# A fixed order list for an attention and two-MLP kernel, a guard in three tasks, norm steps on ScalarE, and a hinted last branch

## The chip, the cores and the metric

The kernel runs on one core of one Trainium2 chip. The metric is the device time of one execution in microseconds (us), as a median over runs; lower is better.

## What is computed

The reference is a gated linear recurrence (four batches, eight heads, 768 tokens, 48 channels a head), and then two MLPs on its output of 768 x 384 a batch. In the first, `u` and `v` are the two halves of `gelu(x @ w_in)`, `v` is normalised over its 512 columns, mixed over the tokens with a 768 x 768 matrix and multiplied by `u`; in the second, a three-tap convolution over the tokens gates the hidden layer.

```python
state = f[:, :, t, :, None] * state + np.einsum('bhd,bhe->bhde', k[:, :, t], v[:, :, t])
y[:, :, t] = np.einsum('bhd,bhde->bhe', q[:, :, t], state)
...
v_n = (v - mu) / np.sqrt(var + 1e-06) * g_ln
v_s = np.einsum('ts,bsd->btd', w_sg, v_n) + b_sg[None, :, None]
x = x + (u * v_s) @ w_out
...
h = np.maximum(x @ w_in2, 0.0)
return (h * sigmoid(conv3(h, conv_w))) @ w_out2
```

## The kernel before

**Stages.** The recurrence is cut into 24 units of 128 tokens, six a batch (`Attention.plan`). A unit runs two scans of the decays on VectorE (`forth`, `back`), scales k and q (`scale`), turns k on TensorE (`turn_k`) and then runs four sets of 32 small matmuls that use a part of the array each: `update`, `states`, `scores`, `values`. They are called the small matmuls below. Its output goes to a DRAM buffer `xd`. Six units make a batch, and `Mlp.first` takes it up: `L` loads a half batch, `vpart` (v0 to v5) makes one block of 128 tokens of v and normalises it, `upart` makes a block of u, `sg` mixes the tokens, `out1` adds the result to `xd` with an accumulating DMA. Every matmul of the MLPs is made of three passes over a high and a low part of its operands (`mm3`), which use the whole array; `split` makes the two parts of an operand, the high one on ScalarE and the low one by a subtraction on VectorE. `sg` needs all six normalised blocks of its batch. `Mlp.second` does the second MLP in eight half batches: eight `in2_part` and three `out2` each.

**Weights.** Weights arrive in double precision. `narrow` brings a piece to single precision in one step on ScalarE and six on VectorE (L577 to L589), each of which reads what the one before wrote. `w_in` has six pieces of 512 columns (0 to 2 for v, 3 to 5 for u), `w_out` four of 384 (13 to 16), the convolution's weights are piece 12, with 24 columns.

**Order.** Nothing is scheduled on the chip. Every operation is a task (`Order.add`) with an engine, a duration, the tasks that it comes after and the ring slots that it takes, and `Order.run` writes the tasks out one by one; an engine executes its instructions in the order written, and waits at each for what it needs. `Order.run` picks the next task by a cost model of its own (`HOP`, `DMA_RATE`, `TABLE_TIME` and a duration for each task) and by due times from a table (`DUE`). PSUM has three banks of a ring `M` for the MLPs and, once the recurrence is done, five of a ring `MA`.

**The norm.** A block's norm goes to and fro between ScalarE and GpSimd: `gelu` with a sum (L906), `mean` on GpSimd (L909), `square` with a sum (L912), `root` in two GpSimd instructions (L918, and the power at L919), `off` on GpSimd (L922), `norm` (L925).

**Guard.** A flag tells whether the products of the decays stayed large enough; if not, a general path recomputes everything. `switch`, one VectorE task, closes the recurrence's memory, reduces the products, and sets the flag. After the last task the flag is read on every engine (L1468), and each engine branches over the general path (L1470).

Of the kernel before, what the change touches and what calls it, by code (L numbers as in the profile page):

```python
# [8 lines left out]
F32 = mybir.dt.float32  # L9
# [14 lines left out]
P = 128  # L24
# [24 lines left out]
HOP = 0.13  # L49

SLACK = 0.2
DMA_RATE, DMA_TIME, TABLE_TIME = 0.21, 1.9, 1.28
# [4 lines left out]
class Hold:  # L57


    def __init__(self):  # L60
        self.left, self.end = 0, 0.0


class Task:
    __slots__ = ("eng", "us", "fn", "after", "rank", "take", "uses", "hold", "table", "kb", "end", "wait", "nexts", "n", "got")


class Order:
# [3 lines left out]


    def __init__(self, rings):
        self.rings = {}
        self.free = dict.fromkeys(("PE", "DVE", "ACT", "POOL", "SP"), 0.0)
        self.dma = 0.0
        self.table = "sigmoid"
        self.ready = {e: [] for e in self.free}
        self.left = 0  # L80
        self.count = 0
        for n, size in rings.items():
            self.ring(n, size)
# [4 lines left out]
    def add(self, eng, us, fn, after=(), rank=0.0, take=(), uses=(), table=None, kb=0.0):  # L88
        t = Task()
        t.eng, t.us, t.fn, t.rank, t.take, t.table, t.kb = eng, us, fn, rank, tuple(take), table, kb  # L90
        t.after = [a for a in after if a is not None]
        t.hold = {n: Hold() for n in t.take}
        t.got = None
# [3 lines left out]
        t.end, t.nexts = None, []  # L97
        t.wait = 0
        for a in t.after:
            if a.end is None:  # L100
                a.nexts.append(t)
                t.wait += 1
        t.n = self.count
        self.count += 1
        self.left += 1
        if not t.wait:
            self.ready[eng].append(t)
        return t

    def start(self, t):  # L110
        at = self.free[t.eng]
        for a in t.after:
            e = a.end + (HOP if a.eng != t.eng or a.kb else 0.0)
            if e > at:
                at = e
        for n in t.take:
            e, _ = self.soonest(n)
            if e is None:
                return None
            if e > at:  # L120
                at = e
        if t.table and t.table != self.table:
            at += TABLE_TIME
        return at

    def soonest(self, name):

        best = None, None
        for n in BANKS if name == "bank" else (name,):
            if n not in self.rings:  # L130
                continue
            slots, i = self.rings[n]
            h = slots[i % len(slots)]
            if h is None:
                return 0.0, n
            if not h.left and (best[0] is None or h.end + HOP < best[0]):
                best = h.end + HOP, n
        return best

    def run(self):  # L140
        while self.left:
            best = None
            for eng, tasks in self.ready.items():
                can = [(at, t) for at, t in ((self.start(t), t) for t in tasks) if at is not None]
                if not can:
                    continue
                soon = min(c[0] for c in can) + SLACK
                at, t = min((c for c in can if c[0] <= soon), key=lambda c: (c[1].rank, c[0], c[1].n))
                if best is None or (at, t.rank) < (best[0], best[1].rank):
                    best = at, t  # L150
            assert best is not None
            self.write(*best)

    def write(self, at, t):
        self.ready[t.eng].remove(t)
        for n in t.take:
            got = self.soonest(n)[1]
            if n == "bank":
                t.got = got
            ring = self.rings[got]  # L160
            ring[0][ring[1] % len(ring[0])] = t.hold[n]
            ring[1] += 1
        t.fn()
        if t.table:
            self.table = t.table
        t.end = at + t.us
        self.free[t.eng] = t.end
        if t.kb:
            self.dma = max(self.dma, at) + t.kb / DMA_RATE / 1000.0
            t.end = self.dma + DMA_TIME  # L170
        for h in t.uses:
            h.left -= 1
            h.end = max(h.end, t.end)
        for x in t.nexts:
            x.wait -= 1
            if not x.wait:
                self.ready[x.eng].append(x)
        self.left -= 1

DUE = {
    "unit load": [
        -548.7, -477.3, -161.3, -153.1, 189.4, 212.0, 364.9, 430.2, 591.1, 816.0, 698.7, 736.9,
        909.1, 1157.3, 1295.0, 1375.7, 1376.1, 1739.4, 1653.8, 1761.4, 3751.4, 2011.8, 2225.9, 3838.8,
    ],
    "unit front": [  # L190
        1385.3, 859.0, 1060.5, -250.2, 1511.2, 1703.3, 1812.9, 2025.9, 2365.2, 229.0, 604.9, 1897.4,
        3788.3, 1201.6, 3779.5, 3805.2, 631.9, 182.0, 1139.5, 3820.9, 1390.5, 1533.0, 2401.4, 499.2,
    ],
    "unit": [
        638.3, 737.0, -203.3, 127.0, 277.0, 425.3, 534.2, 705.8, 1362.3, -576.0, 881.6, 507.0,
        -609.2, -479.0, 1608.3, 211.3, -646.7, -160.9, 210.1, 700.3, 716.4, 533.3, 2213.5, 868.7,
    ],
    "unit out": [
        2412.2, 992.5, 1073.9, 2426.6, 757.2, -615.8, 2198.6, -642.0, 890.0, 1138.3, 1022.7, 1151.8,
        197.2, 624.4, 886.7, 466.3, 991.0, 1980.1, 2189.4, 1392.3, 2317.7, 1151.9, 471.3, 1300.2,  # L200
    ],
    "weight load": [
# [3 lines left out]
    ],  # L206
    "weight": [
# [3 lines left out]
    ],  # L211
    "back load": [
        -436.8, 274.2, 1148.3, 2187.3, 86.8, -537.7, 1513.9,
    ],
    "back": [
        759.7, 289.6, 458.5, 1040.0, 2985.9, -578.4, 1120.4,
    ],
    "item": [
# [10 lines left out]
    ],  # L229
    "item then": [  # L230
# [10 lines left out]
    ],  # L241
    "input load": [
        2182.2, 739.3, 490.0, 530.0, 570.0, 610.0, 650.0, 690.0,
    ],
    "input": [
        706.2, 136.2, 490.0, 530.0, 570.0, 610.0, 650.0, 690.0,
# [1280 lines left out]
```

## Time and profile before

| what | value |
|---|---|
| median of 3 runs | 596.18 us (595.66 to 597.10) |
| the profiled execution | 597.29 us |
| its span, first to last instruction | 595.3 us |
| TensorE busy | 545.9 us, 92% |
| VectorE busy | 440.8 us, 74% |
| ScalarE busy | 362.5 us, 61% |
| GpSimd busy | 67.2 us, 11% |

The span lies inside the execution; the 2.0 us between the two are outside the program. Busy shares are means over stages: the page's row of forty slices has TensorE at 3 to 8 tenths in the first seven and at 9 from the eighth on, and VectorE at 8 or 9 tenths where TensorE is low. The row of the granted TensorE clock has 5 to 9 tenths in the first seven slices and then 9 throughout.

### The profile page before, as it was taken

What the parts mean: (1) busy time and instruction counts of PE and PEld (TensorE: products, weight loads), DVE (VectorE), ACT (ScalarE), POOL (GpSimd) and SP (SyncE); (2) the same over time, 40 slices, a digit from 0 to 9 for tenths busy, and PEclk for the clock granted to TensorE, in tenths of its full rate; (3) what the DMA queues carried; (4) which work ended last, traced back from release to release, by engine and by line L of the source; (5) the groups of instructions that cost most, each with busy time, mean ns of one, the idle gap of its engine ahead of it and who ended that gap; (6) DMA issues with size and microseconds to landing.
All of it is one profiled execution on the core that took longest, in us unless ns stands there. A gap on an engine that the chain in (4) does not pass through costs nothing.

```text
span 595.3 us, 13764 instructions
## 1 busy us (share of the span) xinstructions
PE 545.9 (92%) x5561; PEld 512.3 (86%) x5561; DVE 440.8 (74%) x775; ACT 362.5 (61%) x720; POOL 67.2 (11%) x146
## 2 busy tenths in 40 slices
PE   3553876999999999999999999999999999999995
PEld 2443656998888899889999999999999999999995
DVE  6999898899987987986856344688687685866730
ACT  2534679456788254785347722688777586775830
POOL 2000142000422000333004210110000000000000
PEclk9655897999999999999999999999999999999999
DMA  8687466246858745365334450640210202110011
GB/s 307 185 240 212 116 208 182 79 119 183 210 147 213 215 134 159 102 168 129 106 102 101 122 102 1 149 58 8 81 54 28 71 9 80 36 45 28 14 41 45
DMA packets 56073, 68.33 MB, mean 115 GB/s; under 512 B 26561, under 2 KB 45121, under 8 KB 56001
## 3 DMA queue, kind: packets, MB, share of 16 engines
q1 hardware_dynamic: 52544, 62.64, 34.9%
q0 software_dynamic: 3456, 4.72, 5.6%
q8 instruction: 46, 0.75, 0.5%
q14 instruction: 27, 0.21, 0.1%
HBM read 50.04 MB, written 17.30 MB: 113 GB/s over the span
## 4 chain that ended last, share of the span: by engine, by line
PE 84%; DVE 9%; ACT 2%; POOL 2%; issue 1%; DMA 0%; ACTq 0%; POOLq 0%; DVEq 0%
PE mm L651 44%; PE ma L651 31%; PE at L464 2%; PE at L494 2%; PE at L510 2%; PE at L427 2%; PE pk L413 1%; DVE pr L394 1%; DVE kin L406 1%; DVE pr L381 1%; POOL mv L919 1%; DVE early L589 1%; DVE early L581 1%; DVE sm L434 1%; DVE early L579 1%
## 5 line engine op out<-in xcount | busy, mean ns | idle before, releaser
L1171 DVE SCALAR_TENSOR_TENSOR cv<-h,cols,cv 128x384 f32<-128x384 f32 x128 | 76.0, 616 | 20.0 <-ACT cv L1175 19.4
L651 PE MATMUL mm<-wsg,vn 128*128 128x384 f32 x432 | 82.0, 344 | 0.0
L651 PEld LDWEIGHTS mm<-wsg,vn 128*128 128x128 f32 x432 | 76.4, 192 | 0.9
L651 PE MATMUL ma<-xx,win 128*128 128x386 f32 x378 | 70.3, 338 | 0.0
L651 PEld LDWEIGHTS ma<-xx,win 128*128 128x128 f32 x378 | 66.7, 188 | 0.0
L651 PE MATMUL ma<-wout,gh 128*128 128x384 f32 x224 | 57.4, 337 | 0.0
L651 PE MATMUL mm<-win,x 128*128 128x512 f32 x180 | 48.3, 416 | 0.8 <-ACT x L657 0.8
L651 PE MATMUL mm<-x,win 128*128 128x384 f32 x234 | 46.7, 345 | 1.2 <-ACT win L657 1.0
L662 DVE TENSOR_TENSOR gl<-cv,gh 128x384 fp32r<-128x384 f32 x64 | 35.5, 556 | 16.1 <-ACT gh L657 15.5
L1181 DVE TENSOR_TENSOR cv<-cv,h 128x384 f32<-128x384 f32 x64 | 35.4, 555 | 13.0 <-ACT cv L1178 12.8
L651 PEld LDWEIGHTS mm<-x,win 128*128 128x128 f32 x234 | 40.0, 188 | 2.8 <-ACT win L657 1.4
L1175 ACT ACTIVATE cv<-h,cols 128x384 f32<-128x384 f32 x64 | 39.6, 619 | 3.8 <-DVE gl L662 1.7
L651 PEld LDWEIGHTS mm<-win,x 128*128 128x128 f32 x180 | 33.7, 195 | 8.8 <-ACT x L657 1.1
L651 PE MATMUL mm<-wout,gh 128*128 128x384 f32 x160 | 41.0, 337 | 0.0
L651 PEld LDWEIGHTS ma<-wout,gh 128*128 128x128 f32 x224 | 40.6, 187 | 0.0
L413 PE MATMUL pk<-ident,kin 112*128 112x112 f32 (+1 forms) x96 | 15.8, 294 | 25.3 <-DVE kin L406 18.8
L651 PE MATMUL mm<-xx,win 128*128 128x386 f32 x198 | 38.2, 338 | 0.0
L651 PE MATMUL ma<-wout,gl 128*128 128x384 f32 x112 | 37.7, 337 | 0.0
L651 PE MATMUL mm<-g,wout 128*128 128x384 f32 x192 | 36.6, 340 | 0.0
L657 ACT CAST gh<-cv 128x384 fp32r<-128x384 f32 x64 | 32.5, 508 | 6.2 <-DVE cv L1181 6.1
L651 PEld LDWEIGHTS mm<-xx,win 128*128 128x128 f32 x198 | 35.1, 188 | 0.0
L413 PEld LDWEIGHTS pk<-ident,kin 112*128 112x128 f32 (+1 forms) x96 | 11.1, 150 | 27.5 <-issue 12.3
(120 smaller groups left out, 1127.1 us busy)
## 6 DMA issues: line engine op xcount, KB each, us to landing
kin<-in_kq_pairs SPq DMA_DIRECT2D x24, 512.0 KB, 4.3
stg<-xd SPq DMA_DIRECT2D x16, 576.0 KB, 4.4
ft<-in_f_pairs SPq DMA_DIRECT2D x24, 258.5 KB, 3.4
vt<-in_v_tokens SPq DMA_DIRECT2D x24, 192.0 KB, 3.7
xd<-o SPq DMA_DIRECT2D x96, 48.0 KB, 2.7
stg<-in_moe_w_out SPq DMA_DIRECT2D x12, 384.0 KB, 4.0
xd<-xr POOLq DMA_DIRECT2D x24, 192.0 KB, 4.9
out<-oo SPq DMA_DIRECT2D x24, 192.0 KB, 1.9
```

The costliest lines, as they stand in the source:

```text
L381: self.nc.vector.tensor_tensor_scan(st["pr"][:, 1], st["f"][:, 0:n], self.first, 1.0, op0=ALU.mult, op1=ALU.max)
L413: self.nc.tensor.transpose(pk[:nk, j, 0:R], st["kq"][:, 0, j, 0:nk], self.cst["ident"][0:R, 0:R])
L427: self.nc.tensor.matmul(sc[ts, a, j, :], kt[sl, j, ts], qt[sl, j, ts], start=True, stop=True)
L464: self.nc.tensor.matmul(pu[sl, c, j, :], k2[ts, j, sl], vt[ts, h * D : h * D + D], start=True, stop=True)
L494: self.nc.tensor.matmul(po[g : g + D, c, j, :], state[sl, j, :], st["kq"][sl, 1, j, Q * c : Q * c + Q], start=j == 0, stop=False, skip_gro ...
L510: self.nc.tensor.matmul(po[g : g + D, c, j, :], vt[ts, h * D : h * D + D], sm[ts, a, j, :], start=j == 0 and c == 0 and n == 0, stop=True, ...
L651: self.nc.tensor.matmul(out, l[a], r[b], start=i == 0 and m == 0, stop=i == n - 1 and m == 2)
L657: "ACT", 0.2 + n * 0.0008, lambda: nc.scalar.copy(hi(), src()), after=[after, *wait], rank=rank, uses=uses
L662: lambda: nc.vector.tensor_tensor(lo(), src(), hi(), op=ALU.subtract),
L1171: nc.vector.scalar_tensor_tensor(c, h, self.conv(w, fb), c, op0=ALU.mult, op1=ALU.add)
L1175: nc.scalar.activation(box["c"], box["h"][:, 1 : HALF + 1], AF.Copy, scale=self.conv(1, fb))
L1181: nc.vector.tensor_tensor(box["c"], box["c"], box["h"][:, 1 : HALF + 1], op=ALU.mult)
```

## The change

`Order` no longer plans. The due times and the cost model are gone, and a list `PLACE` of 2,037 task numbers says in which order the tasks are written; where a task takes a bank of either ring, it gets the one whose last user came earliest in that list. The durations and waits that tasks carry are new, but nothing reads them when the kernel is built. In the norm, three one-column steps move from GpSimd to ScalarE, where each follows the big step before it in one task, and GpSimd keeps the power alone. The guard is three tasks: a reduction on VectorE once the products are there, a transpose on TensorE, and the decision on VectorE; opening the second MLP's memory is a task that issues nothing. The flag is read, with a hint that the branch over the general path is likely taken, ahead of the last output copy, and the last output DMA is issued from ScalarE's queue. A second way to do `update` (`sums`) is added and not used (`SUMS` is empty).

```diff
-            for eng, tasks in self.ready.items():
-                can = [(at, t) for at, t in ((self.start(t), t) for t in tasks) if at is not None]
...
+        for count, n in enumerate(PLACE):
+            t = self.tasks[n]
+            assert all(a.done for a in t.after)
...
+PLACE = [
+    0, 22, 1, 554, 2, 23, 44, 3, 24, 4, 25, 5, 6, 7, 8, 66, 46, 45, 555, 26, 544, 9,
+    556, 10, 27, 28, 557, 11, 29, 12, 88, 47, 14, 13, 558, 15, 30, 67, 16, 31, 48, 17, 559, 50,
...
             nc.scalar.activation(box["v"], box["p"], AF.Gelu_apprx_tanh, accum_out=box["s"][:, 0:1])
-        def mean():
-            nc.gpsimd.tensor_scalar(box["s"][:, 1:2], box["s"][:, 0:1], -1.0 / FH, 0.0, op0=ALU.mult, op1=ALU.add)
+            nc.scalar.activation(box["s"][:, 1:2], box["s"][:, 0:1], AF.Copy, scale=-1.0 / FH)
+        def root():
+            t = box["s"][:, 3:4]
+            nc.gpsimd.tensor_tensor(t, t, self.eps[:, 1:2], op=ALU.pow)
...
+            nc.scalar.activation(box["s"][:, 3:4], box["s"][:, 2:3], AF.Identity, bias=self.eps[:, 0:1], scale=1.0 / FH)
...
+            nc.scalar.activation(box["s"][:, 0:1], box["s"][:, 3:4], AF.Copy, scale=box["s"][:, 1:2])
+            nc.scalar.activation(box["v"], box["v"], AF.Identity, bias=box["s"][:, 0:1], scale=box["s"][:, 3:4])
...
+                if r0 + b * S_TOKENS == B * S_TOKENS - P:
+                    self.good = self.read_flag()
                 box["o"] = self.pool2.tile([P, C], F32, tag="oo", bufs=3, name="oo")
...
+            last = r0 + b * S_TOKENS == B * S_TOKENS - P
+            queue = nc.scalar if last else nc.sync
...
+    opened = order.add("ACT", 0.0, switch, after=[t for u in range(N) for t in at.stored[u]])
+    t = order.add("DVE", 0.25, reduce, after=at.ended, rank=("open", 0))
+    t = order.add("PE", 0.2, across, after=[t, opened], rank=("open", 0), take=["MA"])
+    order.add("DVE", 0.45, decide, after=[t], rank=("open", 0), uses=[t.hold["MA"]])
+    def read_flag():
+        tc.mark_branch_hint_location("general", "LikelyTaken", list(mybir.ALL_ENGINES))
+        return nc.values_load(flag, min_val=0, max_val=1)
```

## Rows read from the trace of the kernel before

**Rows 1.** Busy time by stage: stretch, its length, each engine's busy time, clock, DMA share, GB/s

```profile
63.50:97.70 34.20, 26.51 (x517) 20.86 (x516) 31.01 (x60) 27.07 (x58) 11.87 (x22) 1.00 0.55 172
97.70:104.50 6.80, 4.79 (x44) 4.65 (x45) 5.71 (x8) 6.42 (x11) 0.30 (x1) 0.50 0.58 144
104.50:588.40 483.90, 483.46 (x4330) 461.29 (x4328) 348.47 (x622) 300.87 (x597) 51.31 (x104) 1.00 0.36 96
```

**Rows 2.** The same view, from VectorE's first instruction to about the first sg

```profile
4.40:99.10 94.70, 57.55 (x1189) 46.34 (x1189) 87.96 (x149) 53.83 (x110) 12.40 (x26) 0.76 0.69 211
```

**Rows 3.** The merged chain of waits: the first sg (start, length, what)

```profile
100.82 8.16 PE mm L651 x36
```

**Rows 4.** VectorE in order of time, ahead of that sg (start, length, line, operation)

```profile
97.33 0.69 DVE L662 TENSOR_TENSOR vn<-vg,vn 128x512 fp32r<-128x512 f32 x1 [0.49 <-ACT vn L657]
...
99.84 0.69 DVE L662 TENSOR_TENSOR vn<-vg,vn 128x512 fp32r<-128x512 f32 x1 [0.19 <-ACT vn L657]
```

**Rows 5.** VectorE's groups up to 99.1 us (count, busy, mean ns)

```profile
L579 DVE SCALAR_TENSOR_TENSOR stg<-stg 128x384 int32<-128x384 int32 x2 | 1.1, 560 | 0.1
...
L577 DVE TENSOR_SCALAR stg<-stg 128x384 f32<-128x384 f32 x2 | 0.7, 352 | 0.0
...
L580 DVE TENSOR_SCALAR early<-early 128x24 int32<-128x24 int32 x1 | 0.2, 212 | 0.0
```

**Rows 6.** VectorE in order of time: one step, with two kinds of successor

```profile
37.89 0.69 DVE L579 SCALAR_TENSOR_TENSOR early<-early 128x512 int32<-128x512 int32 x1
38.50 0.72 DVE L434 COPY_PREDICATED sm<-seen,at 128x512 f32<-128x512 int32 x1
...
43.55 0.69 DVE L579 SCALAR_TENSOR_TENSOR early<-early 128x512 int32<-128x512 int32 x1
44.28 0.43 DVE L580 TENSOR_SCALAR early<-early 128x512 int32<-128x512 int32 x1
```

**Rows 7.** TensorE in order of time: small matmuls alone and in a row, sg beside them

```profile
119.81 0.67 PE L510 MATMUL at<-sm,vt 64*48 64x64 f32 x32
120.41 3.40 PE L651 MATMUL mm<-wsg,vn 128*128 128x384 f32 x18
123.74 0.68 PE L464 MATMUL at<-vt,k 64*64 64x48 f32 x32
...
126.11 0.26 PE L494 MATMUL at<-kin,new 48*48 48x64 f32 x2
...
126.59 0.65 PE L427 MATMUL at<-kin 48*64 48x64 f32 x32
...
137.11 3.29 PE L651 MATMUL mm<-wsg,vn 128*128 128x384 f32 x18
140.24 0.55 PE L413 MATMUL pk<-ident,kin 112*128 112x112 f32 x4
```

**Rows 8.** The last vpart ahead of the first sg, on TensorE in order of time

```profile
90.43 2.37 PE L651 MATMUL mm<-win,x 128*128 128x512 f32 x9
```

**Rows 9.** The norm's power on GpSimd: duration ns min/median/max

```profile
L919 POOL TENSOR_TENSOR mv<-mv,eps x24: 549/566/2202, 67.6 to 335.3; 128x1 f32<-128x1 f32 x24
```

**Rows 10.** ScalarE in order of time: a table load

```profile
99.83 1.28 ACT L375 ACT_TABLE_LOAD   x1
```

**Rows 11.** ScalarE in order of time: the last output copy

```profile
588.53 0.48 ACT L1212 COPY oo<-mm 128x384 f32<-128x384 f32 x1 [3.71 <-PE mm L651]
```

**Rows 12.** Line 1470, the last branch and the waits behind it, by engine queue

```profile
L1470 SPq EVENT_SEMAPHORE  x8: 17/17/17, 592.0 to 593.6; - x8
...
L1470 ACTq COMPARE_BRANCH  x1: 50/50/50, 589.1 to 589.1; - x1
...
L1470 ACTq EVENT_SEMAPHORE  x1: 17/17/17, 592.1 to 592.1; - x1
```

**Rows 13.** The output DMAs after 560 us, from issue to landing

```profile
DMA to landing us min/median/max: 1.8/1.9/4.3
```

**Rows 14.** DMA issues up to 100 us: count, KB each, median us to landing

```profile
early<-in_moe_w_in SPq DMA_DIRECT2D x6, 512.0 KB, 4.8
```

More of the change, by code (lines that the diff above doesn't have):

```diff
@@ L60, in __init__ @@
     def __init__(self):
-        self.left, self.end = 0, 0.0
+        self.left, self.end = 0, 0
 class Task:
-    __slots__ = ("eng", "us", "fn", "after", "rank", "take", "uses", "hold", "table", "kb", "end", "wait", "nexts", "n", "got")
+    __slots__ = (
+        "n", "eng", "us", "cold", "late", "move", "mode", "fn", "after", "rank", "take", "uses", "hold", "table", "got", "done"
+    )
 class Order:
     def __init__(self, rings):
[L75 to L81, printed above, removed]
+        self.rings, self.tasks = {}, []
         for n, size in rings.items():
@@ L96, in add @@
             h.left += 1
[L97 to L107, printed above, removed]
-        return t
[L110 to L124, printed above, removed]
@@ L154, in write @@
[L154 to L178, printed above, removed]
@@ L185 @@
[L185 to L202, printed above, removed]
[3 rows of a table removed]
-    ],
-    "weight": [
[3 rows of a table removed]
[L211 to L218, printed above, removed]
[10 rows of a table removed]
-    ],
-    "item then": [
[10 rows of a table removed]
[L241 to L246, printed above, removed]
-    ],
-}
@@ new lines, in add, with slot @@
+        t.n, t.got, t.done = len(self.tasks), None, False
+        self.tasks.append(t)
+        return t
+    def slot(self, name):
+        free = None, None
+        for n in BANKS if name == "bank" else (name,):
+            if n in self.rings:
+                slots, i = self.rings[n]
+                h = slots[i % len(slots)]
+                end = 0 if h is None else h.end
+                if (h is None or not h.left) and (free[0] is None or end < free[0]):
+                    free = end, n
+        return free[1]
@@ new lines, in run @@
+    def run(self):
+        assert sorted(PLACE) == list(range(len(self.tasks)))
+        for count, n in enumerate(PLACE):
+            t = self.tasks[n]
+            assert all(a.done for a in t.after)
+            for name in t.take:
+                got = self.slot(name)
+                if name == "bank":
+                    t.got = got
+                ring = self.rings[got]
+                ring[0][ring[1] % len(ring[0])] = t.hold[name]
+                ring[1] += 1
+            t.fn()
+            t.done = True
+            for h in t.uses:
+                h.left -= 1
+                if not h.left:
+                    h.end = count + 1
@@ L253 @@
 SELECTS = set()
+SUMS = set()
 ON_PE = set()
@@ L319, in plan @@
         pr = fw.hold["pr"]
-        rc = add("DVE", 0.18, self.turn, fw, kind="unit front", uses=[pr], take=["last"])
-        pe = add("ACT", 0.2, self.ends, fw, kind="unit front", uses=[pr])
-        bw = add("DVE", 1.23, self.back, rc, kind="unit front", uses=[pr, ft, rc.hold["last"]])
-        kq = add("DVE", 1.23, self.scale, bw, lk, kind="unit front", uses=[pr, kin])
-        self.scaled.append(kq)
-        tr = add("PE", 0.6, self.turn_k, kq, uses=[kin], take=["T"])
-        k2 = add("ACT", 0.53, self.keep_k, tr, uses=[tr.hold["T"]], take=["k2"])
@@ L327, in plan @@
-        up = add("PE", 0.8, self.update, k2, lv, self.scored, uses=[k2.hold["k2"], vt], take=["A"])
-        a1 = up.hold["A"]
-        mid = add("DVE", 0.36, self.middle, up, before, uses=[a1], take=["mid"])
+        rc = add("DVE", 0.1, self.turn, fw, kind="unit front", uses=[pr], take=["last"])
+        pe = add("ACT", 0.1, self.ends, fw, kind="unit front", uses=[pr])
+        self.ended.append(pe)
+        bw = add("DVE", 1.14, self.back, rc, kind="unit front", uses=[pr, ft, rc.hold["last"]])
@@ new lines, in plan @@
+        kq = add("DVE", 1.13, self.scale, bw, lk, kind="unit front", uses=[pr, kin])
+        self.scaled.append(kq)
+        tr = add("PE", 0.38, self.turn_k, kq, cold=0.8, late=0.22, uses=[kin], take=["T"])
+        k2 = add("ACT", 0.43, self.keep_k, tr, uses=[tr.hold["T"]], take=["k2"])
+        if u in SUMS:
+            us, wait = (0.7, None) if before is None else (1.3, before)
+            up = add("PE", us, self.sums, k2, lv, self.scored, wait, cold=1.8 * us, late=0.28, mode="quarter", uses=[k2.hold["k2"], vt], take=["A"])
+            a1 = up.hold["A"]
+            mid = add("ACT", 0.25, self.middle_sum, up, uses=[a1], take=["mid"])
+        else:
+            up = add("PE", 0.46, self.update, k2, lv, self.scored, cold=0.78, late=0.28, mode="quarter", uses=[k2.hold["k2"], vt], take=["A"])
+            a1 = up.hold["A"]
+            mid = add("DVE", 0.27, self.middle, up, before, uses=[a1], take=["mid"])
@@ L330, in plan @@
         md = mid.hold["mid"]
         if before is not None:
-            mid.uses.append(before.hold["new"])
+            (up if u in SUMS else mid).uses.append(before.hold["new"])
             before.hold["new"].left += 1
         if more:
-            new = self.news[u] = add("DVE", 0.72, self.behind, mid, pe, uses=[a1, md], take=["new"])
-        s5 = add("PE", 0.95, self.states, mid, kq, before, uses=[kin, md], take=["A"])
+            if u in SUMS:
+                new = self.news[u] = add("DVE", 0.27, self.behind_sum, up, pe, uses=[a1], take=["new"])
+            else:
+                new = self.news[u] = add("DVE", 0.67, self.behind, mid, pe, uses=[a1, md], take=["new"])
@@ L337, in plan @@
+        s5 = add("PE", 0.45, self.states, mid, kq, before, cold=0.78, late=0.28, mode="quarter", uses=[kin, md], take=["A"])
         a2 = s5.hold["A"]
@@ L347, in plan @@
         else:
-            cm = add("DVE", 0.72, self.seen, s7, uses=[a3], take=["sm"])
-        s6 = add("PE", 0.78, self.values, cm, s5, lv, uses=[a2, cm.hold["sm"], vt])
+            cm = add("DVE", 0.61, self.seen, s7, uses=[a3], take=["sm"])
+        s6 = add("PE", 0.46, self.values, cm, s5, lv, cold=0.83, late=0.28, mode="quarter", uses=[a2, cm.hold["sm"], vt])
         self.stored[u] = []
@@ L656, in split @@
         h = self.S.add(
[L657 removed]
+            "ACT", 0.105 + n * 0.0008, lambda: nc.scalar.copy(hi(), src()), after=[after, *wait], rank=rank, uses=uses
         )
@@ L680, in load @@
             box["steps"][0]()
-        t = S.add("SP", 0.38, load, rank=due("weight load", piece), take=[ring], kb=src.shape[0] * n * 8 / 1000.0, after=after)
+        t = S.add(
+            "SP",
+            0.46,
+            load,
+            rank=due("weight load", piece),
+            take=[ring],
+            kb=src.shape[0] * n * 8 / 1000.0,
+            rate=408.0,
+            after=after,
+        )
         hold = t.hold[ring]
@@ L1079, in fill @@
             kb = n * cols * P * 4 / 1000.0
-            t = S.add("SP", 0.38, load, after=stored + [opened], rank=due("back load", piece + r // n), take=["stg"], kb=kb)
+            t = S.add("SP", 0.46, load, after=stored + [opened], rank=due("back load", piece + r // n), take=["stg"], kb=kb, rate=408.0)
             hi, lo = ((lambda a=a, r=r: parts()[a][:, r : r + n]) for a in range(2))
```

196 lines of the change are left out of this document (103 added, 93 removed), and 117 rows, old and new, of tables (DUE, PLACE).

## The prediction

> **What bounds the kernel now.** I read the stages first. From 104.50 us to 588.40 TensorE is busy for 483.46 of 483.90 us at its upper clock level, 2.4 GHz [rows 1]: once it has work it never waits again, so the end is fixed by when that begins and by how much work is left then. It begins with the first sg, at 100.82 us [rows 3]. Ahead of that VectorE is the engine in use: busy 87.96 of 94.70 us, against 57.55 for TensorE and 53.83 for ScalarE [rows 2]. The last thing that the first sg waits for is a low part of v on VectorE, which ends at 99.84 + 0.69 = 100.53 us [rows 4], 0.29 us before it. So the kernel is a VectorE chain of 100.5 us, then a TensorE chain of 488, then a tail of 595.3 - 588.53 = 6.8 us behind the start of the last copy [rows 11]. Only the first and the last can become shorter by order alone. The middle can become longer.
>
> **The change part by part.** I followed both lists engine by engine and counted. TensorE has the same work ahead of the first sg in both: 54 tasks, six vparts, three uparts, nine units' small matmuls and transposes.
>
> *VectorE's list.* In the list of before 142 tasks stand ahead of the first sg's last need, in the new one 122. The 20 that move behind it are the six steps of w_out's pieces 14 and 16, one low part of w_out, and seven short tasks of the convolution's weights; nothing takes their place. A piece is three steps of about 0.35 and three of about 0.56 us [rows 5], 2.7 us; two are 5.5, the low part 0.55, seven short ones at most 0.21 each, 1.5. That is 7.5; neighbours overlap by some 0.08 us (0.69 long, the next after 0.61 [rows 6]) where neither needs the other, and I take 7.0.
>
> The new list also mixes the steps. A step whose successor reads its result is followed after 44.28 - 43.55 = 0.73 us, one whose successor is independent after 38.50 - 37.89 = 0.61 [rows 6]: 0.12 us for each dependent neighbour. Before has 65 such pairs, 13 of them at tasks that move away; the new list has 17 up to the point below. (65 - 13 - 17) x 0.12 = 4.2 us.
>
> *What binds next.* In the new list the place where VectorE's need runs furthest ahead of TensorE's work is not the first sg but u00, the 48th TensorE task, which needs the low part of w_in's piece 4. Six more tasks of before's 142 come behind that: a low part of 768 columns (by its size 1.5 x 0.69, 1.0), two of v at 0.69 [rows 4], unit 8's mask of 0.72 [rows 6] and its state steps, three instructions of 192 columns, for which I take the 0.35 of a short step [rows 5]. That is 4.1, less six overlaps of 0.08: 3.6. The waits of 0.49 and 0.19 us ahead of low parts of v [rows 4] fall away up to there, as those parts come later. VectorE: 100.53 - 7.0 - 4.2 - 3.6 - 0.7 = 85.0, and u00 starts 0.3 later, at 85.3. This keeps every other idle moment of before.
>
> *What TensorE then has left.* u00 starts 100.82 - 85.3 = 15.5 us before the old first sg, but three uparts and unit 8's four sets of small matmuls are still to do. A upart has half the passes of an sg, which takes 140.24 - 137.11 = 3.13 us between whole-array tasks [rows 7]: 1.57 each. A set alone takes 120.41 - 119.81 = 0.60 [rows 7]. So 4.7 + about 2.3 = 7.0 us come back.
>
> *More hand-overs on TensorE.* An sg between small matmuls takes 123.74 - 120.41 = 3.33 us, 0.20 more than among whole-array tasks; and states followed by scores takes 126.59 - 126.11 = 0.48, where a set alone takes 0.60 [rows 7]. Each separate run of small matmuls costs TensorE about 0.32 us. Behind the first sg there are 45 runs in the old list and 51 in the new: 1.9 us, and 0.6 for the three of unit 8; together 2.5. This is a loss, and nothing hides it.
>
> *The clock.* Before, the first two sg ran with the clock at 0.50, that is 1.2 GHz, from 97.70 to 104.50 [rows 1]: 36 matmuls took 8.16 us [rows 3] where two sg take 6.26 [rows 7], 1.9 us. It fell after a stretch in which TensorE often waited, and had stood at full while TensorE was busy 26.51 of 34.20 us [rows 1]. The new list gives about the same density ahead of u00, so both ends are open, 1.9 gained or 0; I take half, 0.95.
>
> *Norm.* Three GpSimd steps per block go and three one-column steps on ScalarE come. Before, the last vpart ended at 92.80 [rows 8] and its low part at 100.53 [rows 4], 7.7 us later. In the new list the last vpart stands just ahead of u00, and seven tasks, 7.0 us with 0.6 of hand-overs, cover it until the first sg. If the chain loses any of the 7.7 it is covered; unchanged it ends about level. I cost it at nothing.
>
> *Tables.* Table loads on ScalarE rise from 14 to 18. One takes 1.28 us [rows 10], 5.1 in all, behind a ScalarE that is busy 300.87 of 483.90 us [rows 1]; three banks give TensorE at least three uparts, 4.7 us, of cover each time, so nothing in the sum. The Trainium skill, ScalarE: Activation LUTs, section What ACT_TABLE_LOAD costs, gives 1283 ns for the load, as the row has it, but about 2.66 us for a whole switch with a drain; by that ScalarE would lose 10.6 us in all, an estimate, and the sum would still be the same, as one switch would fit the cover; no row shows the drain.
>
> *Guard, banks, tail.* The guard's pieces lie under TensorE's work in both. Banks: 0, as TensorE waited 0.4 us in 484 [rows 1]. The tail: the last copy begins at 588.53 and takes 0.48 [rows 11]; the usual landing is 1.9 us, the longest 4.3 [rows 13]; the last wait of SyncE ends at 593.6 [rows 12], and 1.7 us of closing follow to 595.3. ScalarE's branch starts at 589.1 and its next instruction comes at 592.1 [rows 12]: 3.0 us for a taken branch. In the new order SyncE's branch is free before the last copy, and only ScalarE's stands behind the last output. With the hint effective and a usual landing the tail saves 593.6 - (589.03 + 1.9) = 2.7 us; with 3.0 us of branch on ScalarE after it, about 1.4; with a landing of 4.3 as now, nothing. No row shows a hinted branch; I take 2.0, nearer to the usual landing, and keep 0 to 2.7.
>
> *Sum.* The last copy begins at 588.53 - 15.5 + 7.0 + 2.5 - 0.95 = 581.6. The span ends 6.8 - 2.0 later, at 586.4; with the 2.0 us around the span, 588.4. The profiled execution stood 597.29 - 596.18 = 1.1 above the median; so 587.3.
>
> **Rivals.** *VectorE's remaining idle goes too.* 94.70 - 87.96 = 6.7 us were idle [rows 2], of which I kept all but 0.7. With mixed steps much of it could fill. All but 1.5 of it filled, and the clock warm: 587.3 - 4.5 - 0.95 = 582. Against it: units wait on TensorE and ScalarE in turn, and loads must come sooner.
>
> *The norm chain binds, from a cold clock.* The power on GpSimd took 549 to 2202 ns [rows 9] and stays there. If the last block meets a long one, 1.6 us above the median, and at half clock its vpart takes twice its 2.1, the first sg waits some 3 us: 590 to 592. The Trainium skill, GPSIMD Engine Reference, section Specifications, says that GpSimd shares its SBUF interface with VectorE and contends with some of its instructions; no run here shows that this is what stretches the power.
>
> *The change moves work but not the first sg.* If VectorE is late for other reasons and u00 starts where sg did, less 7.0, only the tail is gained: 595.
>
> *Loads come late; slower.* The new list wants in 85 us what before loaded in 100, at a DMA share of 0.69 [rows 2], hence some 0.8. A piece of w_in takes 4.8 us to land [rows 14], and only two buffers hold such pieces. Every microsecond that VectorE stands ahead of u00 is one at the end. From 597.4 - 587.3 = 10.1 us on the kernel is slower by over 0.2%; three such loads in full, 14 us, give 602, and 598 to 602 is this case. Against it: the first loads of the new list are in the order in which VectorE needs them.
>
> **How the numbers follow.** Two results count as equal within 0.2%, 1.2 us, about what a measurement of this kernel can tell. Chances: forecast, 584 to 590.5, 0.60; idle filled, 580.5 to 584, 0.17; norm and cold clock, 590.5 to 594, 0.09; only the tail, 594 to 595, 0.04; within 0.2%, 0.04; slower by late loads 0.06. So faster 0.90. The low end is 587.3 less all idle (6.0) and less the other half of the clock (0.95), 580.5; the high end takes in the norm and a tail without gain, 594.
>
> **What would show it.** VectorE's last task ahead of u00 near 85 us, hardly any dependent neighbours in narrow's steps; u00 at about 85 and the first sg at 92 to 93 with TensorE full from there; sg's flanked by small matmuls at 3.33; the clock at 1.00 through the first sg; the last copy near 582; no 3 us behind ScalarE's branch. Wrong it would be if VectorE shows waits for DMA ahead of 85 us, if TensorE has gaps behind the first sg, or if the first sg follows its last vpart by more than 8 us.

## The result, and the profile after

The changed kernel takes 588.49 us (median of 4 runs, 587.30 to 591.58) against 596.10 for the kernel before beside it: ratio over the runs 0.989, 95% interval 0.9856 to 0.9923 (the two medians alone give 0.987). The forecast was 587.3, its range 580.5 to 594.0. The profiled execution took 588.64 us, its span is 586.9.

Busy time by stage after, in the columns of [rows 1]: first the two stretches of VectorE's early work, then what lies around and behind the first sg.

```profile
15.00:60.00 45.00, 30.74 (x685) 25.44 (x686) 43.60 (x76) 21.73 (x42) 0.00 (x0) 1.00 0.69 201
60.00:85.75 25.75, 20.15 (x304) 14.96 (x301) 22.39 (x35) 24.27 (x58) 4.00 (x4) 0.93 0.74 210
...
72.90:76.30 3.40, 3.40 (x10) 2.16 (x8) 3.37 (x7) 3.29 (x8) 1.21 (x1) 0.50 0.73 191
...
85.00:97.70 12.70, 10.78 (x170) 9.12 (x170) 7.83 (x18) 12.40 (x27) 1.10 (x2) 1.00 0.40 115
104.50:582.40 477.90, 477.55 (x4284) 454.09 (x4282) 343.93 (x628) 311.04 (x653) 33.50 (x50) 1.00 0.38 98
```

VectorE (third busy number) is full only up to 60 us. From 60 to 97.7 ScalarE (fourth) is the fullest engine, with 24.27 of 25.75 and 12.40 of 12.70 us. TensorE has no idle time worth the name from 104.5 us on, as before. In the record of the granted clock it falls once, from 72.9 to 76.3 us. The 1.00 of the first row disagrees with the durations: a set of small matmuls takes 1.10 us at 55.78 and 0.68 at 88.21 (next view), and in the kernel before, where the record has 0.50 [rows 1], a set at 99.71 takes 1.11. So at 55.78 the matmuls still ran as at the lower level, 1.2 GHz.

TensorE in order of time after, with the idle time ahead of an instruction and its releaser in brackets (rows of other tasks left out):

```profile
55.78 1.10 PE L534 MATMUL at<-sm,vt 64*48 64x64 f32 x32 [1.29 <-DVE sm L422]
...
72.42 3.95 PE L676 MATMUL mm<-win,x 128*128 128x512 f32 x9 [2.08 <-ACT x L682]
...
81.61 2.33 PE L676 MATMUL mm<-win,x 128*128 128x512 f32 x9
83.79 0.68 PE L676 MATMUL mm<-x,win 128*128 128x384 f32 x3
85.06 1.70 PE L676 MATMUL mm<-x,win 128*128 128x384 f32 x6 [0.59 <-ACT win L682]
88.21 0.68 PE L452 MATMUL at<-vt,k 64*64 64x48 f32 x32 [1.44 <-ACT k L406]
...
93.99 1.32 PE L676 MATMUL mm<-wsg,vn 128*128 128x384 f32 x6
...
106.86 3.42 PE L676 MATMUL mm<-wsg,vn 128*128 128x384 f32 x18
110.21 0.26 PE L518 MATMUL at<-kin,new 48*48 48x64 f32 x2
```

Unit 5's last set begins at 55.78 us (67.7 before), u00 at 83.79, the first sg at 93.99. [rows 3] have 100.82 for the first sg, from the merged chain; in the view used here it begins at 100.75:

```profile
100.75 8.23 PE L651 MATMUL mm<-wsg,vn 128*128 128x384 f32 x36
```

Every bracket shown behind 60 us names ScalarE; of those left out the longest is 1.1 us, for a mask on VectorE. The sg between small matmuls takes 110.21 - 106.86 = 3.35 us.

The chain of waits after, merged (start, length, what): it runs mainly on ScalarE from 59.5 us (the norm's power on GpSimd has 1.62 us of it at 75.09 and 0.75 at 80.38), and the second sg hangs on two table loads.

```profile
56.32 3.13 DMA early<-in_w_sg_columns
59.48 0.84 ACT wsg L682
60.33 1.28 ACT L940
...
87.73 0.42 ACT k L406
...
93.53 1.28 ACT L363
94.82 0.64 ACT ft L363
95.46 0.47 ACT o L547
95.95 1.28 ACT L991
97.24 0.50 ACT u L991
97.74 0.04 issue
97.79 3.40 PE mm L676 x18
```

The tail after: ScalarE in order of time, then the line of the last branch by engine queue.

```profile
582.51 0.48 ACT L1244 COPY oo<-ma 128x384 f32<-128x384 f32 x1 [3.64 <-PE ma L676]
583.02 0.38 ACTq L1254 DMA_DIRECT2D out<-oo  x1
```

```profile
L1520 SPq EVENT_SEMAPHORE  x8: 17/17/17, 580.6 to 585.2; - x8
...
L1520 ACTq COMPARE_BRANCH  x1: 68/68/68, 583.4 to 583.4; - x1
L1520 PEldq EVENT_SEMAPHORE  x1: 51/51/51, 583.7 to 583.7; - x1
L1520 ACTq EVENT_SEMAPHORE  x1: 17/17/17, 583.9 to 583.9; - x1
```

ScalarE's branch takes 0.5 us where [rows 12] have 3.0, and SyncE's last wait ends at 585.2, 2.2 us behind the issue of the last output.

The account of the 8.4 us of span: the first sg is 100.75 - 93.99 = 6.76 us earlier; from there to the last copy it is 582.51 - 93.99 = 488.52 instead of 588.53 - 100.75 = 487.78 us, 0.74 longer; the tail is 586.9 - 582.51 = 4.4 instead of 6.8, 2.4 shorter.

### The profile page after: what moved, and what is told of

Its sections match the earlier page's. It is cut to its first block, busy times and chain, and to the rows that moved or that the text cites. A ratio compares the mean times of both kernels' runs of the same rounds, so it can differ in the third digit from the quotient of the medians.

```text
span 586.9 us, 13716 instructions
## 1 busy us (share of the span) xinstructions
PE 549.4 (94%) x5561; PEld 513.4 (87%) x5561; DVE 432.9 (74%) x775; ACT 379.4 (65%) x796; POOL 42.1 (7%) x74
## 4 chain that ended last, share of the span: by engine, by line
PE 83%; ACT 6%; DVE 5%; DMA 3%; issue 2%; POOL 0%; SPq 0%; ACTq 0%; DVEq 0%; POOLq 0%
PE mm L676 45%; PE ma L676 30%; DMA early<-in_moe_w_in 2%; PE at L452 2%; PE at L534 2%; PE at L518 1%; PE at L415 1%; PE pk L401 1%; DVE kin L394 1%; ACT junk L948 1%; ACT vg L940 1%; DVE pr L369 1%; ACT vg L955 1%; ACT wsg L682 1%; DVE sm L422 1%
## 5 line engine op out<-in xcount | busy, mean ns | idle before, releaser
L676 PE MATMUL ma<-xx,win 128*128 128x386 f32 x360 | 65.6, 338 | 0.0
L676 PEld LDWEIGHTS ma<-xx,win 128*128 128x128 f32 x360 | 63.3, 188 | 0.1
L676 PE MATMUL mm<-wout,gh 128*128 128x384 f32 x192 | 49.3, 338 | 0.0
L676 PE MATMUL ma<-wout,gh 128*128 128x384 f32 x192 | 49.2, 337 | 0.0
L1208 ACT ACTIVATE cv<-cv 128x384 f32<-128x384 f32 x64 | 32.7, 522 | 17.8 <-DVE cv L1201 17.5
L676 PEld LDWEIGHTS mm<-xx,win 128*128 128x128 f32 x216 | 38.2, 188 | 0.0
L945 POOL TENSOR_TENSOR mv<-mv,eps 128x1 f32<-128x1 f32 x24 | 17.3, 721 | 257.5 <-ACT mv L951 250.7
L369 DVE TENSOR_TENSOR_SCAN pr<-ft,first 112x516 f32<-112x516 f32 x24 | 29.5, 1229 | 8.3 <-POOL eps L805 4.5
L676 PEld LDWEIGHTS mm<-wout,gh 128*128 128x128 f32 x192 | 34.9, 188 | 0.0
L676 PEld LDWEIGHTS ma<-wout,gh 128*128 128x128 f32 x192 | 34.9, 188 | 0.0
```

Of the source, the lines that this page charges most:

```text
L369: self.nc.vector.tensor_tensor_scan(st["pr"][:, 1], st["f"][:, 0:n], self.first, 1.0, op0=ALU.mult, op1=ALU.max)
L676: self.nc.tensor.matmul(out, l[a], r[b], start=i == 0 and m == 0, stop=i == n - 1 and m == 2)
L945: nc.gpsimd.tensor_tensor(t, t, self.eps[:, 1:2], op=ALU.pow)
L1208: nc.scalar.activation(box["c"], box["c"], AF.Sigmoid)
```

## The experiments

Each kernel was run beside the kernel before; its ratio is to that. The medians of before were 595.18 to 595.92 there, so a few tenths mean nothing. Because the last landing scatters (below), I also give where the last copy begins in the profiled execution: 582.51 in the changed kernel. That place scatters too. Of the kernels made from the changed one none differs from it ahead of 60 us, yet unit 5's last set, at 55.78 in the changed kernel, begins between 54.24 and 55.49 in their profiles. So I also count from that set: the last copy begins 582.51 - 55.78 = 526.73 us behind it in the changed kernel, and u00 ends 86.76 - 55.78 = 30.98 us behind it.

**The tail.** In `e1` the flag is read at the end, unhinted, and the last output leaves from SyncE:

```diff
-                if r0 + b * S_TOKENS == B * S_TOKENS - P:
-                    self.good = self.read_flag()
...
-            queue = nc.scalar if last else nc.sync
+            queue = nc.sync
...
+    m.good = nc.values_load(flag, min_val=0, max_val=1)
-    with tc.If(m.good == 0, label="general"):
+    with tc.If(m.good == 0):
```

> The changed kernel with the ending of before: the flag is read behind the last task and without a hint, and the last output leaves from SyncE's queue. If the tail is worth what the two traces show (6.77 us from the start of the last copy to the end of the span before, 4.39 after), it takes 588.5 + 2.4 = 590.9 us, with the last copy unmoved at about 582.5. If the 6.77 was only a last landing that happened to be long in that one execution, it takes 588.5 to 589.0.

590.72 us, ratio 0.9917 (0.9901 to 0.9933): 2.2 more, as the first theory has it, though the two intervals overlap. The profiled execution was the slowest of the six, 592.81 us, with its span at 591.1:

```profile
85.00:97.70 12.70, 11.26 (x161) 10.01 (x160) 6.53 (x16) 10.99 (x22) 1.10 (x2) 0.73 0.39 109
```

```profile
585.34 0.48 ACT L1242 COPY oo<-ma 128x384 f32<-128x384 f32 x1 [3.64 <-PE ma L676]
```

Here the clock fell between u00 and the first sg (0.73 on the mean), and the last copy came 2.8 us late, though I had expected it unmoved. The tail is 591.1 - 585.34 = 5.8 us, 1.4 more than in the changed kernel, and 1.0 less than in the kernel before: that part of before's 6.8 went with a long landing in its profiled execution. `e4` takes away the hint alone:

```diff
-        tc.mark_branch_hint_location("general", "LikelyTaken", list(mybir.ALL_ENGINES))
```

> The changed kernel without the hint alone; the flag is still read ahead of the last copy and the last output leaves from ScalarE's queue. If the hint shortens a taken branch from 3.0 to 0.5 us: ScalarE's branch at 583.4 ends at 586.4 instead of 583.9, behind the last wait of SyncE at 585.2, so 1.2 us longer, 589.7. If the branch is short for another reason: 588.5.

591.27 us, ratio 0.993 (0.9906 to 0.9953), with 589.44 to 593.13 in six runs. The line of the last branch without the hint:

```profile
L1519 SPq EVENT_SEMAPHORE  x8: 17/17/17, 582.9 to 587.2; - x8
...
L1519 SPq COMPARE_BRANCH  x1: 50/50/50, 580.4 to 580.4; - x1
L1519 PEldq EVENT_SEMAPHORE  x1: 51/51/51, 583.6 to 583.6; - x1
L1519 ACTq COMPARE_BRANCH  x1: 54/54/54, 583.7 to 583.7; - x1
L1519 ACTq EVENT_SEMAPHORE  x1: 17/17/17, 584.1 to 584.1; - x1
```

SyncE's branch takes 2.5 us (580.4 to 582.9) instead of 0.5 with the hint, but ahead of the end, where nobody waits for it; ScalarE's takes 0.4 us without any hint. What is late here is the landing of the last output, 3.7 us. So the first theory falls: the price of the hint that I gave, 3.0 us on ScalarE, does not exist in this order. The second has the branch right and the time wrong. The median is 2.8 us above the changed kernel's, with intervals that overlap; in the one profile the last copy is 0.2 later and the landing 1.8 longer. Whether the hint brings that about stays open.

**The norm.** `e2` puts the three one-column steps back on GpSimd in the new list, `e3` moves them to ScalarE in the old order. `e2`, old and new lines paired by step:

```diff
-            nc.scalar.activation(box["s"][:, 1:2], box["s"][:, 0:1], AF.Copy, scale=-1.0 / FH)
+            nc.gpsimd.tensor_scalar(box["s"][:, 1:2], box["s"][:, 0:1], -1.0 / FH, 0.0, op0=ALU.mult, op1=ALU.add)
...
-            nc.scalar.activation(box["s"][:, 3:4], box["s"][:, 2:3], AF.Identity, bias=self.eps[:, 0:1], scale=1.0 / FH)
+            nc.gpsimd.tensor_scalar(t, box["s"][:, 2:3], 1.0 / FH, LN_EPS, op0=ALU.mult, op1=ALU.add)
...
-            nc.scalar.activation(box["s"][:, 0:1], box["s"][:, 3:4], AF.Copy, scale=box["s"][:, 1:2])
+            nc.gpsimd.tensor_tensor(box["s"][:, 1:2], box["s"][:, 1:2], t, op=ALU.mult)
```

> The changed kernel, same order list, with the norm's three one-column steps back on GpSimd. My prediction costed the move at nothing: 588.0 to 589.0. If ScalarE is what binds from 59 to 88 us, as the chain of waits of the changed kernel says, and its work counts there: six blocks less some 0.5 us each, 585.5 to 587. If the way to GpSimd and back counts, since in this list square stands right behind gelu on ScalarE and must wait for the mean: six blocks with 0.5 to 1 us more each, 591 to 594.

593.26 us, ratio 0.9949 (0.993 to 0.9968), 4.8 above the changed kernel, and the last copy at 586.20, 3.7 later. ScalarE's waits for GpSimd from 59 to 90 us, and on TensorE the fourth vpart and the second upart, in that kernel:

```profile
ACT vg L955 <- POOL mv L947: 5.2, 4, 1.8
...
ACT junk L950 <- POOL mv L941: 0.4, 1, 0.4
```

```profile
73.71 3.30 PE L676 MATMUL mm<-win,x 128*128 128x512 f32 x9 [3.38 <-ACT x L682]
...
90.55 3.25 PE L676 MATMUL mm<-x,win 128*128 128x384 f32 x9
```

ScalarE stands 5.2 us behind GpSimd's last step, and all that is queued behind the norm on ScalarE stands with it: x for the fourth vpart comes so late that TensorE waits 3.38 instead of 2.08 us. The place is `norm` (L955), not `square`: `square` (L950) waits for the mean once, 0.4 us, so the reason in my second theory is not what the trace shows. Counted from unit 5's last set, u00 ends 2.6 us later than in the changed kernel (33.61), with these waits ahead of it. The rest lies behind u00, where the clock fell (the second upart takes 3.25 us instead of 1.83): the first sg follows the end of u00 by 9.26 us instead of 7.23. `e1` has such a fall too, without this edit, so it is not shown that this part belongs to the norm.

`e3` (the same edit the other way round, in the kernel before, whose order stays):

> The kernel before, its own order unchanged, with the three steps on ScalarE. By my prediction (VectorE binds up to the first sg, the norm is covered) nothing: 595.5 to 596.7. If ScalarE's waits for GpSimd (3.8 us in six blocks ahead of the first sg) lay on the path: 592 to 595. If the added work on ScalarE counts: 597 to 600.

596.39 us, ratio 1.0013 (1.0001 to 1.0025): nothing, or a trace slower. So the same edit is worth nothing in the old order and 4.8 us of the median in the new one, of which 2.6 are shown as waits for GpSimd.

**Which engine binds ahead of the first sg.** `e5` and `e6` add work at given tasks, on one engine each:

```diff
+    def extra():
+        nc.vector.tensor_reduce(more[0:R], at.first, axis=AX.X, op=ALU.min)
...
+    order.extra = dict.fromkeys([143, 147, 179, 694, 675, 183, 169], extra)
```

```diff
+    def extra():
+        nc.scalar.copy(m.junk[0:R], at.first[:, 0:FH])
+    order.extra = dict.fromkeys([141, 163, 667, 585, 695, 151, 565, 597], extra)
```

> The changed kernel with seven more reductions of 112x516 on VectorE (about 0.6 us each, 4.2 in all; they read a constant and their result is not used), put between 64 and 79 us. If every microsecond that VectorE has ahead of u00 is one at the end, as my prediction had it: 592.0 to 593.0. If ScalarE binds there and VectorE's 3.4 us of idle between 60 and 85.75 take most of it: 588.5 to 589.7.

590.09 us, ratio 0.9912 (0.9893 to 0.9931), the last copy at 584.26.

> The changed kernel with eight more copies of 112x512 on ScalarE (about 0.5 us each, 4.2 in all; their result is not used), put between 62 and 77 us. If ScalarE's list is what binds from 59 to 88 us: 592.0 to 593.0. If VectorE's list binds, and ScalarE has room: 588.5 to 589.7.

593.08 us, ratio 0.9963 (0.9952 to 0.9974), the last copy at 586.12. The added groups in the two kernels (count, busy, mean ns), and the fourth vpart of the second:

```profile
L1522 DVE TENSOR_REDUCE more<-first 112x1 f32<-112x516 f32 x7 | 4.7, 675 | 0.0
```

```profile
L1521 ACT CAST junk<-first 112x512 bf16<-112x512 f32 x8 | 4.9, 618 | 0.0
```

```profile
74.52 3.70 PE L678 MATMUL mm<-win,x 128*128 128x512 f32 x9 [4.81 <-ACT x L684]
```

4.7 us on VectorE raise the median by 1.6, 4.9 on ScalarE by 4.6. In the profiles, counted from unit 5's last set, the end of u00 moves by 2.7 and 3.6 us, the last copy by 2.95 and 4.62; in `e6` the clock also fell behind u00 (0.66 from 90 to 95 us). ScalarE's list counts more there, but VectorE's is not free: it takes only a part of the added work in its idle time. The reverse, `e12`, makes three of w_sg's high parts on VectorE:

```diff
-                self.split(S_TOKENS, lambda box=box: box["x"], hi, lo, t, k, uses=[t.hold["early"]])
+                self.split(S_TOKENS, lambda box=box: box["x"], hi, lo, t, k, uses=[t.hold["early"]], vec=s in (0, 2, 4))
```

> The changed kernel, same list, with three of the six high parts of w_sg (128x768, 0.82 us each on ScalarE) made on VectorE, where the low part follows. If ScalarE binds from 59 to 88 us and VectorE has room: ScalarE loses 3 x 0.72 = 2.2 us there, VectorE gets 1.5 to 2.5 at the 0.4 us for a microsecond that the added reductions cost: 0.5 to 1.6 us less, 587 to 588. If VectorE binds after all: 589.5 to 591.

590.92 us, ratio 0.9921 (0.9893 to 0.9948), 2.4 above the changed kernel's median, with the last copy at 582.30 and a last landing of 3.9 us in the profile. 60 to 85 us in that kernel:

```profile
60.00:85.00 25.00, 19.93 (x294) 14.98 (x293) 22.62 (x38) 21.49 (x53) 4.99 (x4) 0.86 0.74 213
```

ScalarE is busy 21.49 us where the changed kernel has 23.57, and the last copy is only 0.2 earlier, or 0.26 later if counted from unit 5's last set. Adding to ScalarE costs nearly the whole amount, taking away gives nothing here. What stands right behind ScalarE is not shown; candidates are VectorE, which made the casts instead, and the clock (0.86 here, 0.93 in the changed kernel from 60 to 85 us).

**The clock.** `e7` gives TensorE idle work (16 matmuls ahead of the fourth vpart, 12 ahead of unit 8's update); the first of the two:

```diff
+            if b == 0 and n == 3:
+                for _ in range(16):
+                    nc.tensor.matmul(box["p"][:, : 2 * P], self.warm[:, :P], self.warm, start=True, stop=True)
```

> The changed kernel with idle work on TensorE: 16 matmuls of 128x256 bf16 ahead of the fourth vpart, where TensorE waits 2.1 us, and 12 ahead of unit 8's update, where it waits 1.4 us; the real work overwrites what they write. If the clock falls because of these waits, it stays at 1.00 through the first sg, the fourth vpart takes 2.4 instead of 3.95 us, and the time is 586.5 to 588 with less scatter than the 4 us of the changed kernel. If the clock falls for something else, or the half clock costs nothing because ScalarE binds there: 588 to 589.

588.42 us, ratio 0.9878 (0.9857 to 0.9898), four runs within 588.06 to 588.69. The fourth vpart, and the stretch from 60 to 85 us:

```profile
71.69 2.50 PE L680 MATMUL mm<-win,x 128*128 128x512 f32 x9 [0.23 <-ACT x L686]
```

```profile
60.00:85.00 25.00, 20.23 (x316) 15.24 (x314) 21.64 (x34) 23.32 (x57) 4.03 (x4) 1.00 0.71 211
```

The clock stays at 1.00 (2.4 GHz) and the vpart takes 2.50 instead of 3.95 us. The median stays: a fall at 72.9 us lies beside ScalarE's list. One behind u00 does cost. `e1` is the same kernel up to the tail, and in its profile the clock stayed up at the fourth vpart and fell behind u00. From the top: unit 5's last set, u00's last part, the second upart:

```profile
54.28 1.11 PE L534 MATMUL at<-sm,vt 64*48 64x64 f32 x32 [1.29 <-DVE sm L422]
...
83.57 1.70 PE L676 MATMUL mm<-x,win 128*128 128x384 f32 x6 [0.56 <-ACT win L682]
...
87.75 3.25 PE L676 MATMUL mm<-x,win 128*128 128x384 f32 x9
```

u00 ends 85.27 - 54.28 = 30.99 us behind the set, as in the changed kernel with its fall (30.98) and in `e7` without one (30.98): the fall ahead of u00 costs nothing. But the first sg, at 95.33, follows the end of u00 by 10.06 us, where the changed kernel has 7.23: the fall behind u00 costs 2.8. What puts the fall in one place or the other, in the same code, stays open. The four runs of `e7` lie within 0.6 us, which fits, but four do not show it.

**Moves in the list.** `e8` moves seven tasks, for the three waits seen above (third cast of x, unit 8's turn and keep, its mask, two gelu, unit 9's turn):

```text
PLACE: 691 ahead of 673, 184 ahead of 170, 185 behind 572, 601 behind 191,
       688 and 686 ahead of 200, 206 behind 726
```

> The changed kernel with seven tasks moved in the list: the third cast of x ahead of the second block's norm, unit 8's turn_k ahead of unit 7's values and its keep_k behind the high part of w_in's piece 4, unit 8's mask ahead of a low part of w_sg, two gelu of u ahead of unit 9's decays, and unit 9's turn_k behind the next sg. If TensorE's waits for ScalarE's list (2.1 us ahead of the fourth vpart, 1.4 ahead of unit 8's update, 0.4 ahead of the second sg) are what is left ahead of the end: first sg at 91 to 92.5, 585.5 to 587. If something else is late next: 588 to 589.

587.07 us, ratio 0.9857 (0.9836 to 0.9878): the lowest median here, 1.4 us below the changed one. Its four runs lie below three of the other's four, and the intervals overlap. Unit 5's last set and the first sg in it:

```profile
54.24 1.10 PE L543 MATMUL at<-sm,vt 64*48 64x64 f32 x32 [1.29 <-DVE sm L431]
...
91.61 9.76 PE L685 MATMUL mm<-wsg,vn 128*128 128x384 f32 x54 [0.62 <-ACT u L1000]
```

The first sg begins 2.38 us earlier than in the changed kernel, the last copy, at 580.91, 1.60 earlier. But 1.54 of both were there at unit 5's last set, ahead of every moved task. Counted from it the first sg is 0.84 earlier and the last copy 0.06 (526.67): the profile shows no gain at the end, and with the overlap one is not shown. `e9` moves four more (684 ahead of 715, 605 behind 716, 612 and 719 ahead of 202):

> The list with seven moves, and four more: the first gelu of u ahead of the last block's norm on ScalarE, the convolution's first step behind its cast, and the first sg's scale ahead of unit 9's second scan on VectorE. If TensorE's two waits left in that kernel (0.62 us ahead of the first sg, for that gelu; 0.57 ahead of the fourth sg, for that scale) are the path: 587.1 - 1.2 = 585.9. If others take their place: 587.

587.97 us, ratio 0.9877 (0.9853 to 0.99). The first sg begins at 91.57, by unit 5's last set 1.5 earlier than in the changed kernel, the last copy in the same place (526.74), and another wait has come in place of the one removed:

```profile
105.35 3.42 PE L685 MATMUL mm<-wsg,vn 128*128 128x384 f32 x18 [1.47 <-DVE gt L1031]
```

`e10` is `e9` with the casts of `e12`:

> Eleven moves in the list and three high parts of w_sg on VectorE together. If the two add up: 584.5 to 585.5. If VectorE becomes the bound: no better than the eleven moves alone, 586 to 587.

587.55 us, ratio 0.986 (0.9838 to 0.9882): no better than seven moves. `e11` moves one task more (734 ahead of 224) and puts 14 idle matmuls ahead of unit 7's scores:

> The list with eleven moves, a twelfth (the second sg's scale ahead of unit 10's second scan on VectorE, for which TensorE waited 1.47 us ahead of the fourth sg), and 14 idle matmuls of 128x256 bf16 ahead of unit 7's scores, where TensorE waits 2.2 us and behind which the clock fell. The casts stay on ScalarE, as moving them gave nothing. If the waits and the fall of the clock ahead of about 106 us were what is left: the clock at 1.00 from 60 us on, first sg at 90.5 to 91.5, last copy at 579.5 to 580.5, 585.0 to 586.5 us. If VectorE or ScalarE put the same time into another wait: 587 to 588, as with seven or eleven moves.

589.55 us, ratio 0.9892 (0.9868 to 0.9917); the profiled execution took 587.93. Its stretch behind the first sg:

```profile
105.00:579.00 474.00, 471.86 (x4220) 448.09 (x4219) 342.56 (x626) 310.34 (x653) 34.22 (x50) 1.00 0.37 97
```

```profile
74.84 1.70 PE L422 MATMUL at<-ident 128*128 128x256 bf16 x14 [2.09 <-DVE new L481]
```

The clock is at 1.00 from 60 us on and the first sg at 91.19, but TensorE now waits 2.1 us behind 105 us, 1.4 of them for VectorE in unit 9's states. The idle matmuls came behind the wait that they were to fill (2.09 us, for VectorE), so they could not fill it, and took 1.7 us of their own. Whether they kept the clock up is not shown. In the six runs the mean granted clock splits the times: the three at 1.000 took 587.93 to 589.02 us, the three at 0.993 to 0.996 took 590.08 to 591.14. So a fall still comes in some runs of the same kernel, and goes with some 2 us.

## Why the prediction was right, step by step

| step | predicted | measured |
|---|---|---|
| VectorE's last need of u00 ends | 85.0 | 85.75 |
| u00 ends (85.3 + 1.57) | 86.9 | 86.76 |
| first sg begins (85.3 + 7.0 + 0.6) | 92.9 | 93.99 |
| first sg to last copy | 488.7 | 488.52 |
| last copy begins | 581.6 | 582.51 |
| last copy to end of span | 4.8 | 4.4 |
| profiled execution | 588.4 | 588.64 |
| median | 587.3 | 588.49 |

**VectorE's list: the sum held, the reason only in part.** The low part of w_in's piece 4 ends at 85.75 (85.06 + 0.69), 0.75 us from the sum, and u00 ends 0.1 from where the sum has it. That it is so close is luck: with the same list up to there u00 ends at 85.27 in the profile of `e1` and at 86.03 in that of `e7`. And the sum kept VectorE as the engine that binds up to there. After, that is so only to about 60 us; then the chain of waits lies on ScalarE, VectorE is idle for 3.4 of 25.75 us, and `e5` and `e6` price the two engines, in the median, at 1.6 for 4.7 and 4.6 for 4.9 us. "Every microsecond that VectorE stands ahead of u00 is one at the end" is the sentence that fell.

**The first sg came 1.1 us later** than the sum. The step that failed is what TensorE has left behind u00: I counted its work and not its waits. Unit 8's update waits 1.44 us for `keep_k`, which stands behind a gelu on ScalarE at 87.73, and u00 itself waits 0.59 for the high part of w_in. The prediction had named a sign of being wrong, a first sg more than 8 us behind its last vpart, and it came: 93.99 - (81.61 + 2.33) = 10.05 us. These two waits make 2.0 of the 2.45 us above the 7.6 that it had counted there; the norm chain was not what TensorE waited for.

**The norm at nothing was wrong in the new list.** `e3` bears out the reasoning for the old order (covered). In the new one `e2` shows that list and steps belong together: the norm's last step waits for three GpSimd steps, and everything behind it on ScalarE waits too. The forecast was not hurt, since list and steps came in one change. But the credit for it is not the list's alone, as the sum has it: the list without the steps has a median 2.4 us below before instead of 7.6, and the new tail, worth 2.2 by `e1`, is in it. List and old tail with the old norm were not run, and neither the guard nor the banks alone.

**The clock: the upper end.** I took half of 1.9 us. In the profiled execution the fall came ahead of u00, at 72.9 to 76.3 us, behind TensorE's waits of 0.9 and 2.08 us, where by `e1` and `e7` it costs nothing; the first sg runs at 1.00. So all of the 1.9 came back. This too is luck: in the profile of `e1` the fall came behind u00 and cost 2.8. **The hand-overs** took it again: first sg to last copy is 0.74 longer although 1.9 went, so 2.6 us more, 0.4 of it the wait of the second sg. That leaves 2.2, by subtraction, for hand-overs, where I had 1.9 behind the first sg. The traces have the 45 and 51 runs of small matmuls that I counted in the lists, and an sg takes 3.35 against the 3.33 used.

**Tables at nothing was short by 0.4 us.** Two loads stand 2.4 us apart and the second sg waits for the gelu behind them. The three banks that were to cover a switch were full of u blocks just there. The Trainium skill, ScalarE: Activation LUTs, section What ACT_TABLE_LOAD costs, gives about 2.66 us for a switch with its drain; here the load takes 1.28 and the next instruction begins 0.01 us behind it (93.53 + 1.28 to 94.82), so no drain shows.

**The tail: 2.4 instead of 2.0**, within the 0 to 2.7. The usual landing came, and it, not ScalarE's branch, ends the span. About 1.0 of the 2.4 is the long landing in before's profiled execution, by the tail of `e1`; its median puts the whole tail at 2.2. In the old tail SyncE's branch stands behind the last output: `e1` ends by it, with SyncE's branch at 586.2 and its waits at 588.9 to 589.4.

**The median.** I took 1.1 us off, since the profiled execution before was that much above its median; the one after stands 0.15 above its own. That is nearly all of the 1.2 us between 587.3 and 588.49. With runs from 587.30 to 591.58 of one kernel, and misses of about 1 us in both directions, a forecast within 0.3 us of the profiled execution is partly luck.

Of the rivals, the late loads show as one wait of ScalarE for w_sg on the chain (3.13 us on the chain, for which ScalarE stood idle 0.56) and did not decide; idle time was not filled: it moved to ScalarE's queue.

## What to carry to other kernels

A work-sum of the engine that binds now places the new end well, but the next engine must be priced too: add a few microseconds to one engine at a time and see what the end does. An order list is made for the durations and detours it was written with; an edit that is worth nothing in one list can be worth several microseconds in another. Compare positions in two profiles from a point ahead of the edit, not from the start of the span: here 1.5 us of scatter lay ahead of it. And a long stage brought forward need not end earlier: counted so, 0.84 and 1.5 us at its start became nothing at its end, and in `e9` a longer wait for VectorE stood behind it.

## What the runs showed that I had not expected

The landing of the last output takes two values. Here are the issue rows from 578 us on of the changed kernel and of `e12`, with the same tail:

```profile
out<-oo ACTq DMA_DIRECT2D x1, 192.0 KB, 1.9
```

```profile
out<-oo ACTq DMA_DIRECT2D x1, 192.0 KB, 3.9
```

They are the rows of the last output. With the output on ScalarE's queue it was 1.9 to 2.2 us in eight profiles and 3.7 to 3.9 in three. In these three TensorE's queue came out of its last branch 0.3 to 0.5 us after the output was issued; in the eight it came out 0.6 to 0.7 us after it (as above, 583.7 against 583.02) or ahead of it. The list of DMA queues has instruction fetches in this stretch; one in the way of the output would explain the two values, but that was not tried. It is worth 1.8 us, as much as most edits here. It would explain why `e12`'s median is above the changed kernel's while its last copy is not later, if the long landing came in most of its runs; only one was profiled.

A taken branch took 0.4 to 0.6 us with the hint on all queues but TensorE's (2.7 to 3.9). Without it, it took 2.5 to 3.2 on VectorE and SyncE, but on ScalarE 3.0 in one profile and 0.4 to 0.5 in three, and on GpSimd 0.2 to 0.5.
